# Merging two layer norms, re-cutting weight loads and narrowing a last output tile in a two-layer decode kernel

## The chip, the cores and the metric

The kernel runs on one core of one Trainium2 chip. The metric is the device time of one execution in microseconds (us), as the slowest core shows it; here there is only one. A "profile" is one execution taken by the hardware profiler; "PE" is the matrix engine, "PEld" its weight loads, "DVE" the vector engine, "ACT" the scalar engine, and "SP" the engine that issues the loads.

## The reference, cut to what matters

Two equal layers work on two tokens (`B = 2`) of width `D = 576`. Each layer is attention over a cache of 16384 positions and 32 heads, then a small MLP. Both layers read the same caches and weights.

```python
x = x + attention(LN(x), k_cache, v_cache, wq, wo)   # 2 x 32 heads, 16384 x 128 each
n = LN(x)                                            # input of the MLP block
hs = shift(gelu(LN(n) @ w1)) @ w2                    # of one position only a constant part is left
x1 = n + hs
x  = x + x1 + gelu(LN(x1) @ w3) @ w4                 # w3: 576 x 4608, w4: 4608 x 576
```

With one position per token the shifted term meets only padding, so `hs` doesn't depend on `x`; the kernel computes it once from w2. What matters here: two norms follow each other (`n = LN(x)`, then `LN(n + hs)`), and 1095.6 MB must be read, nearly all of it K and V.

## The kernel before

One SBUF buffer of three "places" takes all that is loaded: K and V of one (batch, head) "unit" fill a place, and between the layers w3, w4 and wq use the same places. An allocator issues a load as soon as the matmuls that read the old content have been queued to signal, in a fixed order. So each load waits for the engines that use what lay there before. Where that wait comes late, the stream of loads runs dry (199 GB/s instead of some 431 in the largest case below); I call this a hole.

```python
W4_PIECES = (1, 4, 4, 2, 1)          # w4 comes in twelfths, in this order, in both layers

def cols(self, ap, t):               # 576 = 4.5 x 128: the last tile takes the LAST 128 columns,
    return ap[:, t*128:(t+1)*128] if t < self.KT - 1 else ap[:, self.D-128:self.D]   # 64 of them twice

def d_matmuls(self, pe, out, w, rhs, first, last):       # one row block of w4, wo or w2
    for t in range(self.KT):                             # KT = 5 output tiles of 128 columns
        ins = pe.matmul(out[:, t*B:(t+1)*B], lhsT=self.cols(w, t), rhs=rhs,
                        start=(first and t == 0), stop=last, skip_group_check=True)

def mlp(self, l):
    self.layernorm(self.xa, "xa", self.xb, "xb")         # n = LN(x): its own sums, Ln/Exp for rstd
    x1 = xb + hs
    self.layernorm(self.x1, "x1", self.xn, "xn")         # LN(x1): sums again
    xsum = xa + x1
    ...                                                  # w3, gelu, then w4: 36 blocks x 5 tiles = 180 matmuls

def ncp(self, l, i): return self.NCH // 2 + 1            # of 16 chunks of K, PE takes 9, DVE 7

rows("wq", 1, self.wq, [third, third + n, third + 2*n, third + unit, third + unit + n])
# attention, layer 2, first units ("early"): exponentials at chunk 3, weighing with V at chunk 5
# ... (cut: loop machinery, softmax, transposes, projection pieces)
```

## Time and profile before

| | before |
|---|---|
| time, median of 4 runs | 2563.47 us (2563.23 to 2563.85) |
| profiled span | 2563.0 us |
| bytes read | 1095.64 MB at 427 GB/s |
| PE, DVE, ACT busy | 64%, 69%, 48% |
| DMA engines busy in the slices | 9 tenths or more, except the last |

The page's slices (40 equal slices of 64 us: busy tenths of the DMA engines, then what they moved) show what bounds the kernel before:

```profile
DMA  9999999999999999999999999999999999999998
GB/s 410 429 431 433 432 430 432 432 431 431 431 431 433 431 432 432 432 430 431 427 378 429 428 433 431 433 431 434 430 431 432 431 433 431 431 433 432 430 431 370
```

No compute engine is near full, but the DMA engines are busy from end to end. The stream moves 429 to 434 GB/s except in the first slice, in slices 20 to 23 (counted from 1) where the layers meet, and in the last. The windows view of before has for each stretch: length, busy us of each engine (number of instructions), granted PE clock (as a share of full speed), DMA share and GB/s.

```profile
core 0: us, PE busy (x) PEld busy (x) DVE busy (x) ACT busy (x) POOL busy (x), PEclk, DMA share, GB/s
1284.00:1290.00 6.00, 4.86 (x163) 4.67 (x163) 0.45 (x4) 0.60 (x3) 0.00 (x0) 0.50 0.63 199
1302.00:1307.00 5.00, 2.95 (x67) 2.66 (x65) 1.09 (x7) 0.50 (x2) 0.00 (x0) 0.50 0.94 357
1308.00:1312.00 4.00, 1.91 (x64) 1.75 (x63) 0.00 (x0) 0.00 (x0) 0.00 (x0) 0.50 1.02 420
1326.00:1330.00 4.00, 2.12 (x25) 1.85 (x25) 3.93 (x7) 2.21 (x3) 0.00 (x0) 0.50 0.89 328
1338.00:1342.00 4.00, 4.00 (x83) 4.00 (x81) 3.93 (x6) 2.15 (x4) 0.00 (x0) 0.50 0.71 233
1500.00:2500.00 1000.00, 635.43 (x14241) 591.50 (x14239) 693.80 (x1005) 484.61 (x765) 0.00 (x0) 0.67 1.00 431
```

Lost stream time is length x (1 - GB/s / 431.8), where 431.8 is the steady rate that I read from the loops. So 199 GB/s over 6 us is a loss of 3.2 us; the stretches at 1302, 1326 and 1338 lose 0.9, 1.0 and 1.8. Between 1500 and 2500 us next to nothing is lost: 0.6 us by the DMA records. The timeline of PE between the layers (start, duration, line, operation, output<-inputs, shapes, count, [idle before <- what ended it]) shows the two norms:

```profile
1278.31 0.29 PE L649 MATMUL misc<-otn,wolast 128*128 128x2 bf16 x5 [0.26 <-DVE otn L843]
1279.06 0.61 PE L579 MATMUL misc<-xa,small 128*128 128x16 f32 x2 [0.46 <-DVE xa L574]
1279.60 0.59 PE L581 MATMUL misc<-xa,small 64*128 64x4 f32 x2
1282.10 0.61 PE L579 MATMUL misc<-x,small 128*128 128x16 f32 x2 [1.91 <-DVE x L574]
1282.64 0.59 PE L581 MATMUL misc<-x,small 64*128 64x4 f32 x2
1284.73 1.12 PE L613 MATMUL sps<-xn,buf 128*128 128x2 bf16 x36 [1.51 <-DVE xn L597]
```

The last projection (1278.31) is followed by a pair of fp32 sums at 1279.06 and another pair at 1282.10; only at 1284.73 can the first w3 matmul start.

```profile
2551.66 1.76 PE L649 MATMUL misc<-prod,buf 128*128 128x2 bf16 x60 [0.45 <-DMA buf<-in_B_w_dram]
2555.82 1.76 PE L649 MATMUL misc<-prod,buf 128*128 128x2 bf16 x60 [2.41 <-DMA buf<-in_B_w_dram]
2557.91 0.96 PE L649 MATMUL misc<-prod,buf 128*128 128x2 bf16 x30 [0.33 <-DMA buf<-in_B_w_dram]
2559.16 0.56 PE L649 MATMUL misc<-prod,buf 128*128 128x2 bf16 x15 [0.29 <-DMA buf<-in_B_w_dram]
```

The last load ends at 2559.11, and only 15 matmuls and some small steps come after it: the output is issued 2.3 us after the last landing. The 60 matmuls of a w4 piece take 1.76 us (29 ns each) and hide between the landings of the pieces. The granted clock in this stretch was 0.50.

### The profile page before, as it was taken

To read this page: it belongs to the slowest core of one execution; us is meant where nothing else is said; L and a number is where in the kernel's file an instruction comes from. 1 tells how busy PE (TensorE), PEld (TensorE's weight loads), DVE (VectorE), ACT (ScalarE), POOL (GpSimd) and SP (SyncE) were. 2 spreads that over 40 slices of the span, in tenths; PEclk is the share of its full clock that TensorE was granted. 3 is DMA by queue.
4 is the path that set the end of the run, shared out by engine and by line. 5 is a ranking of instruction groups with operands and counts; after the bars stand their busy time and mean duration, and the time that the engine had idled before them with its cause. 6 is when DMAs were issued, how large, how long until landed. Compare 5 with 4: busy or idle time off the path is not lost.

```text
span 2563.0 us, 83950 instructions
## 1 busy us (share of the span) xinstructions
PE 1645.9 (64%) x36813; PEld 1532.6 (60%) x36813; DVE 1756.7 (69%) x2592; ACT 1226.3 (48%) x1941; POOL 1.0 (0%) x12
## 2 busy tenths in 40 slices
PE   5666666666566656666668766666666666666666
PEld 5555655566565656655668766556655665565555
DVE  5676767677666766766648867766776767677664
ACT  4544544454445445544436555444544544454442
POOL 0000000000000000000000000000000000000000
PEclk8766666666667666766656667666766666666666
DMA  9999999999999999999999999999999999999998
GB/s 410 429 431 433 432 430 432 432 431 431 431 431 433 431 432 432 432 430 431 427 378 429 428 433 431 433 431 434 430 431 432 431 433 431 431 433 432 430 431 370
DMA packets 46935, 1096.37 MB, mean 428 GB/s; under 512 B 4964, under 2 KB 6056, under 8 KB 11560
## 3 DMA queue, kind: packets, MB, share of 16 engines
q1 hardware_dynamic: 46888, 1095.66, 99.7%
q8 instruction: 39, 0.64, 0.1%
q14 instruction: 8, 0.07, 0.0%
HBM read 1095.64 MB, written 0.00 MB: 427 GB/s over the span
## 4 chain that ended last, share of the span: by engine, by line
DMA 60%; issue 16%; DVE 15%; PE 8%; ACT 0%; SPq 0%; DVEq 0%
DMA buf<-in_A_k_cache_dram 58%; DVE prod L778 12%; PE tps L749 5%; DVE sd L781 3%; PE misc L797 2%; DMA buf<-in_B_w_dram 1%; PE ops L821 1%; DMA buf<-in_A_wq_dram 0%; DVE small L799 0%; PE sps L766 0%; PE sps L613 0%; ACT ktsb L753 0%; SPq L431 0%; PE misc L649 0%; PE misc L579 0%
## 5 line engine op out<-in xcount | busy, mean ns | idle before, releaser
L753 ACT ACTIVATE ktsb<-tps 128x1024 bf16<-128x1024 bf16 x1152 | 1119.4, 1032 | 873.0 <-PE tps L749 868.4
L749 PE MATMUL tps<-ident,buf 128*128 128x128 bf16 x9216 | 903.0, 262 | 623.5 <-DMA buf<-in_A_k_cache_dram 612.3
L749 PEld LDWEIGHTS tps<-ident,buf 128*128 128x128 bf16 x9216 | 727.9, 120 | 651.7 <-DMA buf<-in_A_k_cache_dram 631.7
L781 DVE TENSOR_REDUCE sd<-prod 128x8 f32<-128x1024 bf16 x896 | 1093.2, 1220 | 31.0
L778 DVE TENSOR_TENSOR prod<-buf,qb 128x1024 bf16<-128x1024 bf16 x896 | 610.7, 682 | 11.1 <-DMA buf<-in_A_k_cache_dram 10.2
L821 PE MATMUL ops<-p,buf 128*128 128x1 bf16 x16384 | 463.0, 165 | 69.5 <-DMA buf<-in_A_v_cache_dram 60.8
L821 PEld LDWEIGHTS ops<-p,buf 128*128 128x128 bf16 x16384 | 445.2, 101 | 79.2 <-DMA buf<-in_A_v_cache_dram 69.9
L799 DVE TENSOR_REDUCE small<-misc 128x1 f32<-128x128 f32 x128 | 37.3, 292 | 647.6 <-PE misc L797 647.6
L766 PE MATMUL sps<-qcur,ktsb 128*128 128x1 bf16 x9216 | 395.5, 166 | 112.1 <-ACT ktsb L753 87.7
L766 PEld LDWEIGHTS sps<-qcur,ktsb 128*128 128x128 bf16 x9216 | 345.6, 101 | 176.2 <-ACT ktsb L753 170.8
L733 ACT ACTIVATE qb<-misc 128x128 bf16<-128x128 f32 x130 | 36.0, 277 | 373.6 <-PE misc L730 373.6
L797 PE MATMUL misc<-identS,small 128*128 128x128 f32 x256 | 95.0, 475 | 9.8 <-DVE small L791 9.7
L797 PEld LDWEIGHTS misc<-identS,small 128*128 128x128 f32 x256 | 69.8, 333 | 11.6 <-DVE small L791 11.4
L807 ACT ACTIVATE p<-sps,small 128x72 bf16<-128x72 f32 x128 | 41.6, 325 | 6.7 <-DVE small L799 6.7
L807 ACT ACTIVATE p<-sd,small 128x56 bf16<-128x56 f32 x128 | 44.8, 350 | 0.0
L725 ACT ACTIVATE qcur<-qt 128x1 bf16 (+1 forms) x130 | 29.7, 228 | 20.3 <-DVE qt L659 20.3
L730 PE MATMUL misc<-ident,qcur 128*128 128x128 bf16 x130 | 34.8, 268 | 1.3 <-ACT qcur L725 1.3
L876 PE MATMUL misc<-lpiece,small 128*128 128x16 f32 x28 | 8.5, 385 | 40.9 <-DVE lpiece L874 40.9
L876 PEld LDWEIGHTS misc<-lpiece,small 128*128 128x128 f32 x28 | 7.0, 311 | 43.5 <-DVE lpiece L874 43.5
L787 DVE TENSOR_REDUCE small<-sps 128x1 f32<-128x72 f32 x128 | 28.5, 222 | 0.9 <-PE sps L766 0.9
L807 ACT ACTIVATION_READ_ACCUMULATOR p<-sps,small (+1 forms) x128 | 27.3, 214 | 0.0
L807 ACT ACTIVATION_READ_ACCUMULATOR p<-sd,small (+1 forms) x128 | 26.7, 209 | 0.0
(88 smaller groups left out, 222.2 us busy)
## 6 DMA issues: line engine op xcount, KB each, us to landing
buf<-in_A_k_cache_dram SPq DMA_DIRECT2D x124, 4096.0 KB, 24.3
buf<-in_A_v_cache_dram SPq DMA_DIRECT2D x122, 4096.0 KB, 33.6
buf<-in_A_v_cache_dram SPq DMA_DIRECT2D x5, 2048.0 KB, 22.5
buf<-in_B_w_dram SPq DMA_DIRECT2D x8, 1152.0 KB, 30.8
buf<-in_A_wq_dram SPq DMA_DIRECT2D x8, 1024.0 KB, 8.3
buf<-in_A_wo_dram SPq DMA_DIRECT2D x14, 576.0 KB, 34.6
buf<-in_B_w_dram SPq DMA_DIRECT2D x4, 1728.0 KB, 20.6
buf<-in_A_k_cache_dram SPq DMA_DIRECT2D x3, 2048.0 KB, 10.8
```

The lines of the kernel that those rows point to most:

```text
L725: self.act(lambda a, u: a.activation(out=self.qcur[:, q:q + 1], in_=self.qt[:, bass.ds(u, 1)], func=ACT.Copy), r=["qt"], w=[f"qcur{q}"], u ...
L730: self.pe(lambda pe: pe.matmul(self.misc[:, 0:128], lhsT=bcast(self.qcur[:, q:q + 1], 128), rhs=self.ident[:, :], start=True, stop=True), ...
L733: self.act(lambda a: a.activation(out=self.qb[q][:, :], in_=self.misc[:, 0:128], func=ACT.Copy), r=["P:misc"], w=[f"qb{q}"])
L749: ins = pe.transpose(self.tps[b][:, j * 128:(j + 1) * 128], kt[:, (j0 + j) * 128:(j0 + j + 1) * 128], self.ident[:, :])
L753: self.act(lambda a: a.activation(out=self.ktsb[k][:, :, :].rearrange("p a b -> p (a b)"), in_=self.tps[b][:, :], func=ACT.Copy), r=[f"P:t ...
L766: ins = pe.matmul(self.sps[sp][:, col:col + 1], lhsT=self.ktsb[k][:, j, :], rhs=self.qcur[:, sp:sp + 1], start=True, stop=True)
L778: self.dve(lambda v: v.tensor_tensor(out=self.prod[d][:, :, :], in0=k3, in1=bcast_mid(self.qb[q][:, :], self.CH), op=ALU.mult), r=[*res, f ...
L781: self.dve(lambda v: v.tensor_reduce(out=self.sd[q][:, o:o + self.CH], in_=self.prod[d][:, :, :], axis=AX.X, op=ALU.add), r=[f"prod{d}"], ...
L797: self.pe(lambda pe: pe.matmul(self.misc[:, 128:256], lhsT=bcast(self.m[:, q:q + 1], 128), rhs=self.identS[:, :], start=True, stop=True), ...
L799: self.dve(lambda v: v.tensor_reduce(out=self.bias[:, q:q + 1], in_=self.misc[:, 128:256], axis=AX.X, op=ALU.max, negate=True), r=["P:misc ...
L807: self.act(lambda a, u, c0=c0, c1=c1, src=src: a.activation(out=self.p[q][:, c0:c1], in_=src, func=ACT.Exp, bias=self.bias[:, q:q + 1], sc ...
L821: ins = pe.matmul(self.ops[q][:, 0:1], lhsT=vt[:, j * 128:(j + 1) * 128], rhs=self.p[q][:, h * self.TB + j:h * self.TB + j + 1], start=(h ...
```

## The change

The intent: shorten what lies between the layers, so that the loads that wait for it are issued earlier, and let the stream run through. In the words of the change: both MLP layer norms from one round of sums, w4 and wq in finer pieces at new places, PE takes more chunks of layer 2's first units. (The pieces are finer for layer 1's w4 alone: layer 2's w4 gets a larger first piece, five twelfths, and wq stays in five rows at new places.) The diff, cut to its core:

```diff
-    W4_PIECES = (1, 4, 4, 2, 1)
+    W4_PIECES = ((1, 2, 3, 3, 2, 1), (5, 4, 2, 1))          # by layer
...
-                rows("wq", 1, self.wq, [*(third + k * n for k in range(KT - 2)), third + unit, third + unit + n])
+                free = third + (self.FA - self.W4_PIECES[0][0]) * self.FJ * D
+                rows("wq", 1, self.wq, [free, *(third + k * n for k in range(KT - 1))])
...
+    def layernorms(self):        # sums of xa, xa*hs and xa*xa at once; hs's own sums are made once, with w2
+        ...                      # var(x1) = var(n) + 2 cov(n, hs) + var(hs), from those sums
...
     def d_matmuls(self, pe, out, w, rhs, first, last):
         for t in range(self.KT):
-            ins = pe.matmul(out[:, t * self.B:(t + 1) * self.B], lhsT=self.cols(w, t), rhs=rhs,
+            lo = 0 if t < self.KT - 1 else self.p0                       # p0 = 64
+            ins = pe.matmul(out[lo:128, t * self.B:(t + 1) * self.B], lhsT=w[:, t * 128:(t + 1) * 128 - lo], rhs=rhs,
                             start=(first and t == 0), stop=last, skip_group_check=True)
...
     def ncp(self, l, i):
-        return self.NCH // 2 + 1
+        return self.NCH // 2 + (3, 2)[min(i, 1)] if l == 1 and i < 2 else self.NCH // 2 + 1
...
-                if i >= 1 and c == (3 if early else 4):                  # exponentials
+                if i >= 1 and c == (2 if early else 4):
-                if early and c == 5:                                     # weighing
+                if early and c == 4:
-            if l == 0 and i == 1:
+            if l == 0 and i == 0:
                 self.shift_term()                                        # w2, hs and its sums
...
-        self.dve(lambda v: v.tensor_copy(out=self.xn[:, :, :], in_=self.xa[:, 0, :, :]), r=["xa"], w=["xn"])
+        # (the last cast: layer 2's MLP now writes xn itself)
```

The last output tile of `d_matmuls` is now 64 columns wide, written to partitions 64 to 127. The merged sums need this: the 64 padding rows stay zero, and one fp32 sum over all 128 rows suffices.

## The prediction

> **What bounds it now.** The load stream. The page shows the DMA engines at nine tenths in every slice, 1095.6 MB read at 427 GB/s over 2563.0 us; the inner slices hold 430 to 433. At 431.8 GB/s (my reading of the steady loop) the bytes alone need an estimated 2537 us. The other 26 us are start (4 us), tail, a slow drift, and holes where the two layers meet (slice 20: 378 GB/s). The windows view in small steps puts the holes, as lost stream time, at: 1284 to 1290 us, 3.2 us (w4's second piece waits until two w3 rows have been multiplied, issued 1287.06); 1302 to 1307, 0.8 us (wq waits for w4's buffers, first row issued 1297.26); 1326 to 1330, 1.1 us (K of layer 2's fourth unit waits for VectorE's sixth dot of the first unit, issued 1326.90); 1338 to 1342, 2.1 us (V of that unit waits for the first unit's weighing, issued 1338.92). Sum 7.2 us. Nothing else in the loops is lost: PE, VectorE and ScalarE work there is off the critical path.
>
> **What the change does.**
> 1. One round of sums. The timeline has 5.9 us from the last addition to xa (1278.8) to the first w3 matmul (1284.7), two norms of about 3.0 us each. The merged chain has one fp32 sum (0.6 us instead of two at 1.2, twice), about nine small VectorE steps of 0.2 us and two Ln/Exp pairs of 0.5 us: estimate 3.5 us. Gain 2.3 us, needed only in layer 1; in layer 2's MLP the PE waits for w4's transfers anyway.
> 2. w4's second piece now waits for one w3 row (1.1 us earlier). With 1, issue at about 1283.6 instead of 1287.1; the first hole shrinks to about 0.6 us.
> 3. wq's first row goes to a place free after w4's first piece, the others behind small pieces: issue near 1291, hole gone. In exchange layer 2's K now waits for wq's second and third row; perhaps 0.3 us.
> 4. PE takes 11 and 10 chunks in layer 2's first units; VectorE has 5 and 6 dots of 1.86 us. K's issue comes about 2 us earlier after the unit's start: that hole goes. The weighing comes 2.5 us earlier, but the stream is further ahead too: about 1 us of that hole stays.
> 5. w2 and its statistics at unit 0: some 2 us more of small work in a phase with slack of over 10 us; free. Last cast dropped: 0.2 us at the tail.
>
> **Expected gain.** 7.2 - (0.6 + 0.3 + 1.0) + 0.2 = 5.5 us in mean stream time. [...] the last w4 piece's sixteen signals spread over 5.9 us (2553.2 to 2559.1). [...] I take 0.3 us off.
>
> Predicted 2558.2 us, 8 in 10 between 2556.0 and 2560.8. Faster by over 2%: 0.01; within 2%: 0.985; slower: 0.005.
>
> **Right or wrong in the profile.** Step 1: last xa addition to first w3 matmul about 3.5 us. Step 2: over 350 GB/s in the stretch that held 103 to 174. Step 3: wq's first row issued before w4's last piece has landed. Step 4: VectorE dots of the first unit end about 9.5 us after its first transpose. Steady slices unchanged, PE busy slightly up, VectorE slightly down.
>
> **What would make it wrong.** Engine spread at the tail eating the gain; a new wait at layer 2's K; [...] layer 1's second unit delayed enough to starve the stream.

The sum came to 7.2 - 1.9 + 0.2 = 5.5 us; less the 0.3 us it is 5.2, and 2563.47 - 2558.2 is the 5.3 us that I use below. The reason for the 0.3 us rested on a link between holes and spread that no trace shows. So the 0.3 us are only my guess, beside the 5.9 us of spread that the trace does show.

## More of the kernel before

The weights are the stationary operand (`lhsT`), and the moving operand has two columns (the two tokens). In the trace of before, w4's 128x128 tiles take PE 29 ns each (60 in 1.76 us), so I count PE's time there by weight tiles.

The chain of waits (what ended last, in order of time: start, duration, what) and PE's timeline show the end of the kernel:

```profile
2539.29 19.83 DMA buf<-in_B_w_dram
...
2559.16 0.57 PE misc L649 x15
...
2560.19 0.74 PE misc L561 x5
...
2560.95 0.45 DVE prod L565
```

## The result, and the profile after

The changed kernel is correct and takes 2564.26 us (median of 4 runs, 2563.55 to 2566.16) against 2563.47 us. The ratio is 1.0004, with a 95% interval from 0.9987 to 1.0021: the same. (Ratios here are the mean time of one kernel's fast runs over that of the other's of the same rounds, so not quite the ratio of the medians.) The prediction, 2558.2 us with a range of 2556.0 to 2560.8, missed: none of the 5.3 us came.

Yet the stream did gain. The page's GB/s line and the windows view of after:

```profile
GB/s 409 430 431 433 431 430 433 432 431 432 430 433 432 431 432 431 433 431 431 426 408 431 428 432 430 432 433 431 432 432 430 432 431 431 433 432 431 430 433 341
```
```profile
core 0: us, PE busy (x) PEld busy (x) DVE busy (x) ACT busy (x) POOL busy (x), PEclk, DMA share, GB/s
1284.00:1290.00 6.00, 4.11 (x136) 3.94 (x133) 0.16 (x1) 0.02 (x1) 0.00 (x0) 0.50 0.97 373
1302.00:1307.00 5.00, 3.11 (x45) 2.73 (x42) 1.04 (x7) 0.50 (x2) 0.00 (x0) 0.50 1.01 424
1308.00:1312.00 4.00, 3.02 (x108) 2.88 (x106) 0.10 (x1) 0.00 (x0) 0.00 (x0) 0.50 0.80 275
1326.00:1330.00 4.00, 3.73 (x69) 3.59 (x67) 2.71 (x4) 3.80 (x8) 0.00 (x0) 0.78 1.00 426
1338.00:1342.00 4.00, 3.35 (x71) 3.05 (x69) 2.08 (x6) 3.31 (x5) 0.00 (x0) 1.00 1.07 455
```

Here the hole of 1284 to 1290 went from 199 to 373 GB/s (a loss of 0.8 us instead of 3.2), and those of 1302, 1326 and 1338 are gone. A new one is there, 1308 to 1312, with 275 GB/s instead of 420: 1.5 us. From the trace's DMA records, the loss from 1262 to 1348 us is 4.0 us instead of 8.7. The last landing came at 2554.52 instead of 2559.11, 4.6 us earlier. The merged sums are as fast as predicted:

```profile
1279.09 0.40 PE L693 MATMUL misc<-otn,wolast 128*128 128x2 bf16 x5 [0.26 <-DVE otn L892]
1279.97 0.64 PE L587 MATMUL misc<-xhs,small 128*128 128x30 f32 x2 [0.47 <-DVE xhs L619]
1283.07 1.16 PE L655 MATMUL sps<-xn,buf 128*128 128x2 bf16 x36 [2.47 <-DVE xn L593]
```

From the end of the last addition (1279.70) to the first w3 matmul (1283.07) are 3.4 us, against 5.9 before. So the gain was there until the last load had landed, and was lost after it. The chain of waits and PE's timeline at the end of after:

```profile
2547.21 0.14 issue
2547.34 12.30 PE misc L693 x180
...
2560.65 0.45 DVE prod L573
```
```profile
2542.10 0.64 PE L666 MATMUL sps<-xnh,buf 128*128 128x4 bf16 x18 [0.34 <-DMA buf<-in_B_w_dram]
2547.34 12.29 PE L693 MATMUL misc<-prod,buf 128*128 128x2 bf16 x180 [4.61 <-DMA buf<-in_B_w_dram]
```

PE waits 4.61 us for the first w4 piece, now five twelfths, which lands at 2547.21. Then the 180 matmuls of w4 run in one block of 12.29 us, 68 ns each instead of 29. The last piece landed at 2554.52, in the middle of this block. The granted clock was 0.50 here too, so the clock is not the reason. The end is no longer bound by the load, but by PE: the output is issued 6.6 us after the last landing instead of 2.3.

Why did the same 180 matmuls take so much longer? The tile view of the weight loads lists their shapes, with the least, median and greatest ns of one (it counts every second one of the 360):

```profile
L693 PEld LDWEIGHTS misc<-prod,buf x360: 103/106/126, 1292.0 to 2559.4; 128*128 128x128 bf16 x144, 128*64 128x64 bf16 x36
```

36 of each layer's 180 weight tiles are now 64 columns wide, one in each group of five. The single instructions in the two traces (not a view of the page; start times and gaps, in ns, worked out from the records):

```
before, one group after another:  128 128 128 128 128 | 128 ...    gap to the next start: 26 to 28 each
after, from 2548.005:             128 -49-> 128 -27-> 128 -27-> 128 -95-> 64 -142-> 128   sum 340 per group of five
```

The narrow tile starts 95 ns after the one ahead, and the next wide one 142 ns after it; the one after that takes 49 ns. A group of five takes 340 ns instead of 133. The time is lost at both starts, 95 and 142 ns where 27 are usual; what PE does in it the trace does not show, and whether it is the change of width or the narrow tile itself that costs, a trace of this kernel alone cannot say.

Two theories were to be told apart. Theory A: the narrow tile makes w4 slow, and this eats the stream's gain at the tail. Theory B: the tile is hidden where the stream is the limit, and the gain is lost to the sixteen DMA engines' spread, to new holes, or to the test form.

### The profile page after: what moved, and what is told of

It is laid out like the page before. It is cut to its first block, busy times and chain, and to the rows that moved or that the text cites. A ratio compares the mean times of both kernels' runs of the same rounds, so it can differ in the third digit from the quotient of the medians.

```text
span 2562.7 us, 84020 instructions
## 1 busy us (share of the span) xinstructions
PE 1671.5 (65%) x36847; PEld 1559.0 (61%) x36847; DVE 1751.6 (68%) x2595; ACT 1231.3 (48%) x1944; POOL 1.0 (0%) x12
## 4 chain that ended last, share of the span: by engine, by line
DMA 59%; issue 16%; DVE 13%; PE 10%; ACT 1%; SPq 0%; DVEq 0%
DMA buf<-in_A_k_cache_dram 56%; DVE prod L827 11%; PE tps L798 6%; DMA buf<-in_B_w_dram 1%; DVE sd L830 1%; PE misc L846 1%; DMA buf<-in_A_v_cache_dram 1%; PE ops L870 1%; ACT ktsb L802 1%; PE misc L693 1%; DMA buf<-in_A_wq_dram 0%; PE sps L815 0%; SPq L435 0%; PE sps L655 0%; ACT p L856 0%
## 5 line engine op out<-in xcount | busy, mean ns | idle before, releaser
L693 PE MATMUL misc<-prod,buf 128*128 128x2 bf16 (+1 forms) x360 | 24.6, 179 | 6.6 <-DMA buf<-in_B_w_dram 4.6
L693 PEld LDWEIGHTS misc<-prod,buf 128*128 128x128 bf16 (+1 forms) x360 | 22.4, 111 | 8.8 <-issue 4.7
## 6 DMA issues: line engine op xcount, KB each, us to landing
buf<-in_A_k_cache_dram SPq DMA_DIRECT2D x3, 2048.0 KB, 11.2
```

The costliest lines, as they stand in the source:

```text
L693: ins = pe.matmul(out[lo:128, t * self.B:(t + 1) * self.B], lhsT=w[:, t * 128:(t + 1) * 128 - lo], rhs=rhs, start=(first and t == 0), stop ...
```

## The experiments

The kernels as given wait, inside their loops, for semaphore values held in registers. Such kernels were not admitted to the chip for experiments. So each experiment uses one of three test forms of the same program, and is compared with a before and an after in the same form:

- `_u`: the loops are written out, so that all waits are against constants.
- `_c`: the loops are kept. All engines meet once per turn of two units: SP waits for each engine's count of the turn, takes it back, and gives each a go signal. The semaphores of K, V and wo are taken back to zero before each use.
- `_d`: as `_c`, but the last turn of each loop is written out after it, for a reason that the second job showed.

```diff
 # _u
-        self.s.loops.append((l * U + first, (U - first) // 2, 2, self.WO_PIECE, ...))
 # _c, on SP, once per turn
+            for s, n in subs: eng.wait_ge(sems[s], n)
+            for s, n in subs: eng.sem_inc(sems[s], -n)
+            for e in engines: eng.sem_inc(sems["go_" + e], 1)
 # _d, ahead of all that
+        self.loops = [(first, n - 1, *more) for first, n, *more in self.loops]
```

"Wide" puts the last tile back and zeroes the padding rows ahead of each sum. "Batched" keeps 64 columns, but does all wide tiles of a piece before its narrow ones. "Narrow" is the kernel before with nothing but the narrow tile.

```diff
 # wide: the changed kernel with before's tile
-            lo = 0 if t < self.KT - 1 else self.p0
-            ins = pe.matmul(out[lo:128, ...], lhsT=w[:, t * 128:(t + 1) * 128 - lo], rhs=rhs,
+            ins = pe.matmul(out[:, ...], lhsT=self.cols(w, t), rhs=rhs,
+        # and ahead of each sum over xa or hs:
+        self.dve(lambda v: v.memset(self.xa[0:self.p0, KT - 1, :], 0.0), r=["xa"], w=["xa"])
 # batched: the changed kernel, order of the tiles alone (w4 and the three-head projection)
-                for j in range(n * self.FJ):
+                for ts in (range(KT - 1), (KT - 1,)):
+                  for j in range(n * self.FJ):
 # narrow: the kernel before, with
-            ins = pe.matmul(out[:, ...], lhsT=self.cols(w, t), rhs=rhs,
+            lo = 0 if t < self.KT - 1 else self.p0
+            ins = pe.matmul(out[lo:128, ...], lhsT=w[:, t * 128:(t + 1) * 128 - lo], rhs=rhs,
```

### First job: loops written out

> The kernel before with its loops written out (the looped form waits on registers, which the check refuses). Nothing else differs. All theories: the same computation and the same loads, plus the instruction fetches of some 84,000 instructions: 2590 to 2625 us. The gap from the landing of w4's last piece to the end stays near 3.9 us and w4's last three pieces keep PE waiting on the loads. This run is the baseline of the other written-out kernels.

> The changed kernel with its loops written out. All theories: within about 3 us of before_u (the looped pair differs by 0.8 us). The 180 w4 matmuls of layer 2 take 12.3 us in one run and the end comes 7 to 8 us after w4's last piece has landed, as in the looped one.

> after_u with the last output tile of every down-projection 128 columns wide again (as before), the 64 padded rows zeroed by one memset ahead of the sums. Theory A (the 64-wide matmul between 128-wide ones makes each group of five cost 340 ns instead of 135, and that ate the gain): the 180 w4 matmuls take 5 to 5.6 us, the end comes 4 us after the last landing, the time is 3.5 to 5.5 us below after_u. Theory B (the larger first w4 piece of layer 2, 5 twelfths landing 2.6 us after the gelu is ready, ate it): the time stays within 1.5 us of after_u. Theory C (the loads themselves end late because of the engines' spread): w4's last landing moves and the rest does not follow.

> after_u, still with the 64-wide last tile, but in w4 and in the three-head projection all 128-wide matmuls of a piece come first and its 64-wide ones after them, so that the width changes twice a piece instead of twice a group of five. Theory A1 (the change of width costs): w4 in 5.3 to 6.5 us, time within 1 us of wide_u. Theory A2 (a 64-wide matmul is slow by itself): w4 stays above 9 us, time within 1.5 us of after_u.

| run | median us (range) | ratio to before [95%] | last w4 landing, output issued | after it |
|---|---|---|---|---|
| before_u | 2612.01 (2611.24 to 2612.76) | 1.0189 [1.0172, 1.0206] | 2605.88, 2608.18 | 2.3 us |
| after_u | 2612.25 (2611.27 to 2613.49) | 1.0189 [1.0172, 1.0206] | 2602.79, 2609.36 | 6.6 us |
| wide_u | 2609.24 (2607.16 to 2610.15) | 1.0176 [1.0159, 1.0193] | 2603.67, 2605.77 | 2.1 us |
| batched_u | 2609.39 (2607.63 to 2609.89) | 1.0176 [1.0159, 1.0193] | 2603.78, 2606.14 | 2.4 us |

All are correct, as are all kernels of the later jobs. The kernel before, beside them, took 2563.88 us, so the form itself costs 48 us. Writing the loops out took the instruction fetches from 39 to 288 (before_d, with loops again, has 48). The DMA queue lines of the pages of before and before_u (packets, MB, share of the 16 engines):

```profile
q8 instruction: 39, 0.64, 0.1%
```
```profile
q8 instruction: 288, 4.72, 0.7%
```

An estimate from these lines, 4.08 MB more at the 431.8 GB/s of the steady stream, is 9.4 us. What the rest of the 48 us is was not measured. But the form keeps the picture: after is level with before, its last landing comes 3.1 us earlier, and the tail gives it back. With the tile back to 128 columns, or with the narrow tiles put together, the tail is as short as before's. PE's timeline of batched_u:

```profile
2596.57 2.63 PE L693 MATMUL misc<-prod,buf 128*128 128x2 bf16 x75 [4.59 <-DMA buf<-in_B_w_dram]
2600.66 3.98 PE L693 MATMUL misc<-prod,buf 128*128 128x2 bf16 x105 [1.47 <-DMA buf<-in_B_w_dram]
```

The 75 matmuls of the first piece, 15 narrow ones among them, take 2.63 us instead of the 5.1 that 75 x 68 ns would make. In the records the wide ones start every 27 ns, the first narrow one 95 ns after, and the narrow ones then every 53 ns. So in batched order a group costs 4 x 27 + 53 = 161 ns, and of the 340 ns in the changed order some 179 come with the two changes of width. Narrow tiles are the slower ones even in a row, 53 against 27 ns; whether that is their load is not shown. (A narrow load itself is recorded with a median of 157 ns in batched_u and 125 ns in after, against 104 and 105 for a wide one; but loads overlap, as wide tiles start every 27 ns.) This part, 26 ns a group, is small beside the 179. wide_u and batched_u beat before_u by 2.8 and 2.6 us; since the intervals of the ratios overlap, this job alone does not settle the size. Two expectations missed narrowly: wide_u came 3.0 us below after_u instead of 3.5 to 5.5, and batched_u's w4 took PE 6.6 us instead of at most 6.5.

### Second job: loops kept, one meeting per turn

> The kernel before, with its loops kept but waiting on constants: the engines meet once per two units and the counts are taken back there. The instruction stream is as short as in the kernel before, so the fetches of the written-out kernels are gone. All theories: within 3 us of the kernel before (2561 to 2567 us), because the engines wait for K at each unit's start anyway; w4's last landing about 4 us before the end.

> The changed kernel in the same form. All theories: within 2 us of before_c, w4's 180 matmuls of layer 2 in 12.3 us, w4's last landing about 4 us earlier than in before_c and the end 7.6 us behind it.

> after_c with the 128-wide last tile. Theory A (the changes of width in the down-projections took the gain): w4 in 5 to 5.6 us of PE, the end about 3.3 us behind the last landing, 4 to 6 us below both before_c and after_c, 2557 to 2560 us. Theory C (the spread of the DMA engines took it): 0 to 2 us below after_c.

> before_c with nothing of the change but the 64-wide last tile. Theory A: layer 2's w4 pieces take PE 4.1 us per four twelfths instead of 1.8, so that PE falls behind the landings: w4 ends about 3.3 us later, and between the layers xa comes 3 to 3.5 us later, of which 1 to 2 us reach the load stream: 3 to 6 us above before_c. Theory B (the large first piece is what hurts, the width only in company with it): within 1.5 us of before_c.

| run | median us (range) | ratio to before [95%] |
|---|---|---|
| before_c | 2568.30 (2566.81 to 2568.50) | 1.0017 [1.0003, 1.0030] |
| after_c | 2578.40 (2577.74 to 2580.34) | 1.0056 [1.0043, 1.0070] |
| wide_c | 2570.21 (2570.09 to 2570.81) | 1.0025 [1.0012, 1.0039] |
| before_narrow_c | 2577.78 (2576.96 to 2578.77) | 1.0055 [1.0041, 1.0068] |

The tile alone costs before 9.5 us, and taking it out of after gains 8.2: both more than expected (3 to 6 and 4 to 6), and in both pairs the intervals of the ratios are apart. But before_c came 4.6 us above the kernel before, where under 3 were expected, after_c came 10.1 us above before_c instead of within 2, and wide_c came out 1.9 us *above* before_c, where it should have been 4 to 6 us below. The waits of PE in the last stretch of before_c, and of after_c, show why:

```profile
PE misc L903 <- PEq L248: 8.5, 1, 8.5
```
```profile
PE misc L952 <- PEq L248: 19.3, 1, 19.3
```

PE sat 8.5 us (before_c) or 19.3 us (after_c, and wide_c too) at the gate that ends the loop. SP gives that signal, but SP was held in issuing loads for 25 to 33 us; it got to the signal after three of w4's five last loads in before_c, but only after all four in after_c and wide_c. This is a fault of my test form, not of either kernel. It also laid all 180 w4 matmuls bare behind the gate, so the tile cost its full 7.3 us at the tail (12.32 against 4.97 us in the chains of after_c and wide_c). In before_narrow_c, whose gate wait (8.4 us) is that of before_c, the rest is in the stream: between 1262 and 1348 us it lost 11.2 us instead of 7.9. So with w4 in the pieces of before, the tile costs the stream between the layers too. The form was changed so that nothing waits for SP there.

### Third job: the last turn of each loop written out

> The kernel before with the loops kept and constant waits, like before_c, but with the last turn of each loop written out after the loop. In the earlier form the traces showed that the first small matmul of the last unit's softmax waited 8.5 us (before_c) and 19.3 us (after_c, wide_c) for SP's go signal, while SP was held for 25 to 33 us in issuing DMAs; so its tails say nothing. Here no go signal is needed there. Both theories: 2564.0 to 2566.5 us, output DMA issued 2.0 to 3.0 us after w4's last landing.

> The changed kernel in the same form. Theory A (the 64 columns wide last tile makes w4's 180 matmuls last 12.3 us instead of 5.0, and this eats the stream's gain at the tail): within 1.5 us of before_d, w4's last landing 3.5 to 5 us earlier than in before_d, output DMA issued 6 to 7.5 us after it. Theory B (the tile is hidden where the stream is the limit; the gain is lost to the engines' spread and to new holes): also near before_d, but the last landing is no earlier than before_d's by more than 1.5 us.

> The changed kernel, only the last tile back to 128 columns. Theory A: 3.5 to 5.5 us below before_d and after_d, output DMA issued 2.0 to 2.6 us after w4's last landing, the hole before layer 2's K (wq's second row waits for the MLP's end) under 1 us. Theory B: within 1 us of after_d.

> The changed kernel with the narrow tile kept, only layer 2's w4 pieces back to 1, 4, 4, 2, 1 twelfths (the change has 5, 4, 2, 1). Theory A says that the tail is bound by PE: from the first piece's landing to the end of 180 matmuls. PE idled 4.6 us in the changed kernel until 5 twelfths had landed; with 1 twelfth first it starts after gelu: 2.0 to 2.6 us below after_d, and still 1.5 to 3 us above wide_d. Theory B: within 0.7 us of after_d.

```diff
 # after_w4l2_d, the changed kernel with
-    W4_PIECES = ((1, 2, 3, 3, 2, 1), (5, 4, 2, 1))
+    W4_PIECES = ((1, 2, 3, 3, 2, 1), (1, 4, 4, 2, 1))
```

| run | median us (range) | ratio to before [95%] | stream loss 1262 to 1348 | last w4 landing, output issued | after it |
|---|---|---|---|---|---|
| before_d | 2566.21 (2565.59 to 2566.66) | 1.0009 [0.9996, 1.0023] | 8.6 us | 2559.84, 2562.15 | 2.3 us |
| after_d | 2566.41 (2565.36 to 2567.55) | 1.0009 [0.9995, 1.0022] | 4.7 us | 2556.52, 2563.16 | 6.6 us |
| wide_d | 2561.12 (2560.77 to 2561.76) | 0.9989 [0.9976, 1.0003] | 4.7 us | 2555.93, 2558.03 | 2.1 us |
| after_w4l2_d | 2565.19 (2564.53 to 2566.56) | 1.0006 [0.9992, 1.0020] | 4.1 us | 2555.55, 2561.14 | 5.6 us |

Now before_d and after_d stand to each other as the real kernels do, with the same tails (2.3 and 6.6 us). Theory A's numbers came, but for one: after_d's last landing was 3.3 us earlier than before_d's, where 3.5 to 5 were expected. With the tile alone put back, wide_d is 5.3 us faster than after_d and 5.1 us faster than before_d, with ranges that lie 3.6 us or more apart. (The intervals of the ratios still touch, at 0.9995 to 1.0003; that the tail is what differs is read from the traces.) Stream loss and landing of wide_d are those of after_d within what single traces scatter (see the fourth job); what differs clearly is the tail. Theory B wanted wide_d within 1 us of after_d, and it falls. wide_d's chain of waits and PE timeline end like before's:

```profile
2536.66 19.27 DMA buf<-in_B_w_dram
...
2555.98 0.57 PE misc L801 x15
```
```profile
2548.78 2.14 PE L801 MATMUL misc<-prod,buf 128*128 128x2 bf16 x75 [4.63 <-DMA buf<-in_B_w_dram]
2552.82 1.55 PE L801 MATMUL misc<-prod,buf 128*128 128x2 bf16 x52 [1.91 <-DMA buf<-in_B_w_dram]
2554.67 1.86 PE L801 MATMUL misc<-prod,buf 128*128 128x2 bf16 x53 [0.30 <-issue]
```

The load is the last wait again, and PE idles between pieces. One expectation missed: the hole before layer 2's K should have been under 1 us in wide_d; it was 1.1 us by the DMA records. In after_d it was 1.3 us, so the tile has little to do with this hole.

after_w4l2_d gained 1.2 us in the median (2.0 in the profiled runs; the ranges overlap), less than the 2.0 to 2.6 expected, and stayed 4.1 us above wide_d, where 1.5 to 3 were expected. PE's timeline says why:

```profile
2545.76 1.09 PE L800 MATMUL misc<-prod,buf 128*128 128x2 bf16 x15 [2.01 <-DVE prod L830]
2548.29 11.36 PE L800 MATMUL misc<-prod,buf 128*128 128x2 bf16 x165 [1.44 <-DMA buf<-in_B_w_dram]
```

The small first piece lets only 15 matmuls run early (1.09 us). The other 165 wait for the second piece (landed 2548.24), which is hardly earlier than the large first one. So the larger first piece cost about the time of those 15 matmuls. That the tail is bound by PE is confirmed; the waiting time of 4.6 us was not all to be had.

### Fourth job: the single steps, and one improvement

The cause was found, but not whether each term of the predicted sum was right. Each of these kernels is wide_d with one step undone, or with one more.

> wide_d (the changed kernel with the last tile back to 128 columns) with one more edit: layer 2's first loaded K comes in four quarters instead of a half and two quarters, so its first piece waits for one row of wq to have been multiplied, not for two. In wide_d the stream lost 1.1 us between 1310 and 1314 us, and K's first piece was issued at 1310.71, 2.5 us after the matmuls of the row before had ended (1308.2). Theory C (the row of wq that K's place waits for is what empties the stream there): K's first issue near 1308.3, loss in the stretch 1308 to 1316 under 0.4 us, time 0.6 to 1.3 us below wide_d, so 2559.8 to 2560.5. Theory D (that stretch is lost to the end of the MLP, the sums before wq, whatever K waits for): same loss, time within 0.4 us of wide_d.

> wide_d with two norms, each with its own sums, one after the other, in the MLP; all else as in wide_d. Last addition to xa until first w3 matmul: near 6 us instead of 3.5. If the prediction's first step is right, layer 1's hole near 1285 grows by 2.0 to 2.6 us and the time by as much (2563.1 to 2563.8); in layer 2 nothing is lost, as PE waited 4.6 us for w4 there. If other holes take it up: less than 1.2 us.

> wide_d with layer 1's w4 in the pieces of the kernel before (1, 4, 4, 2, 1 twelfths) and wq's rows for layer 2 in the places of before (steps 2 and 3 of the prediction undone; layer 2's w4 stays). The prediction's terms: hole after the first w4 piece +2.6 us, wq's hole +0.8, K's new hole -0.3 (measured in wide_d: 1.1). Sum with the measured hole: 2.0 to 2.6 us slower than wide_d (2563.1 to 2563.7). If less than 1 us: the places bought little, and the merged sums did most.

> wide_d with PE's share of layer 2's first two units back to 9 of 16 chunks and the exponentials and weighing at their old places (step 4 undone). The prediction's terms: hole of K +1.1 us, of V +1.1 us (one of its 2.1 us was to remain). In wide_d neither hole is left (losses of 1326 to 1330 and 1336 to 1342 together under 0.3 us), so the undone step should cost up to 3.2 us, and more than before's, as the stream is further ahead: 2.2 to 4 us slower than wide_d (2563.3 to 2565.1). If under 1.5 us, those holes had come from the stream's place in time, not from the share of chunks.

```diff
 # wide_k2_d: layer 2's first loaded K in quarters
-                kv("K", l, i, {(1, 2): (2, 1, 1), (1, 3): (2, 2)}.get((l, i)))
+                kv("K", l, i, {(1, 2): (1, 1, 1, 1), (1, 3): (2, 2)}.get((l, i)))
 # wide_ln2_d: layernorms() as two norms, each with its own sums (one fp32 sum each, not before's two)
 # wide_places_d
-    W4_PIECES = ((1, 2, 3, 3, 2, 1), (5, 4, 2, 1))
+    W4_PIECES = ((1, 4, 4, 2, 1), (5, 4, 2, 1))
-                rows("wq", 1, self.wq, [free, *(third + k * n for k in range(KT - 1))])
+                rows("wq", 1, self.wq, [*(third + k * n for k in range(KT - 2)), third + unit, third + unit + n])
 # wide_chunks_d: ncp() is NCH // 2 + 1 everywhere; exponentials at chunk 3, weighing at chunk 5
```

| run | median us (range) | ratio to before [95%] | stream loss 1262 to 1348 | against wide_d: stream, time |
|---|---|---|---|---|
| wide_k2_d | 2561.19 (2560.60 to 2563.16) | 0.9990 [0.9976, 1.0004] | 4.3 us | -0.4, +0.1 us |
| wide_ln2_d | 2563.14 (2561.59 to 2563.47) | 0.9996 [0.9982, 1.0009] | 6.5 us | +1.8, +2.0 us |
| wide_places_d | 2562.35 (2561.37 to 2562.91) | 0.9994 [0.9980, 1.0008] | 5.4 us | +0.7, +1.2 us |
| wide_chunks_d | 2563.54 (2563.01 to 2565.61) | 1.0000 [0.9986, 1.0014] | 6.2 us | +1.5, +2.4 us |

These ran in another job than wide_d, on another chip, where the kernel before took 2563.46 instead of 2563.87 us, and the 95% intervals overlap. So the times are good to about half a microsecond. The stream losses are from one trace each, and they scatter too: up to 1308 us wide_d, wide_k2_d and wide_chunks_d are the same program, yet from 1262 to 1308 us they lost 3.2, 2.2 and 2.4 us. So a difference under about 1 us shows nothing, and wide_d's trace, which lost most there, makes the others look better than they are. What the steps are worth has to be read where the kernels differ:

- The two norms in a row lost 4.5 us up to 1308, that is 1.3 to 2.3 us more than those three, and 2.0 us in time: the first step was right, near the lower end of what was expected. From the last addition to the first w3 matmul took 5.0 us, not near 6 as expected (wide_d 3.5, before 5.9), so this edit undoes some three fifths of the step.
- The chunks lost 3.8 us from 1308 to 1348, 2.3 us more than wide_d, in holes at 1326 and 1336 to 1342 that came back, and 2.4 us in time. That is the 2.2 us of the prediction's terms; the whole window shows only 1.5 because of the scatter before 1308.
- The places fell short: 2.0 to 2.6 us were expected, and 1.2 us came in time. In wide_places_d wq's hole came back (0.9 us at 1302 to 1306), but K's hole of 1.1 us went away in exchange. From 1284 to 1294 us it lost 2.5 us, against 2.2 in wide_d, and 1.4 and 1.6 in wide_k2_d and wide_chunks_d, so what the small pieces saved is not clear of the scatter.

The windows view of wide_d, and then of wide_k2_d, tells what K's hole was made of, and where its end led:

```profile
1310.00:1312.00 2.00, 0.69 (x26) 0.60 (x23) 0.00 (x0) 0.00 (x0) 0.00 (x0) 0.50 0.98 338
1312.00:1314.00 2.00, 1.55 (x48) 1.44 (x48) 0.00 (x0) 0.00 (x0) 0.00 (x0) 0.50 0.84 326
1336.00:1338.00 2.00, 1.11 (x17) 1.11 (x17) 1.97 (x3) 0.19 (x2) 0.00 (x0) 0.50 1.17 492
```
```profile
1310.00:1312.00 2.00, 0.55 (x20) 0.46 (x18) 0.00 (x0) 0.00 (x0) 0.00 (x0) 0.50 1.01 391
...
1336.00:1338.00 2.00, 0.59 (x7) 0.59 (x6) 1.97 (x4) 0.55 (x1) 0.00 (x0) 0.50 0.74 295
```

With K in quarters its first piece was issued at 1307.64 instead of 1310.71, and the hole from 1308 to 1316 shrank from 1.2 to 0.6 us (under 0.4 was expected): that fits theory C, that K waited for wq's rows. But the time did not move, where 0.6 to 1.3 us were expected. The stream met a new hole at V (1336 to 1338, 295 GB/s); from 1308 to 1348 us, where alone the two kernels differ, it lost 2.1 us against 1.5, so in all nothing was gained. That it met V's wait because it was further ahead is likely, not shown. In its profiled run, the slowest of its five, the last load's sixteen signals also spread over 8.5 us instead of 6.7. Whether the spread grows when holes go stays open: it was 5.9 us before, 6.1 after, 6.6, 7.4 and 6.7 us in before_d, after_d and wide_d, and 10.1 us in wide_u.

No kernel in the four jobs beats wide_d. It is 5.1 us faster than before_d in the same form, and 2.8 us faster than the kernel before itself (2563.87 us in the same job; the ratio's interval, 0.9976 to 1.0003, just includes 1), although its form costs about 2.3 us (before_d against before). Worked out from these, an estimate for the changed kernel in its own form with only the tile put back is 2563.5 - 5.1 = 2558.4 us.

## Why the prediction was wrong

In the prediction's own terms, what failed is the path at the tail. Its sum counts stream time alone and lets the end follow the last landing, since "in layer 2's MLP the PE waits for w4's transfers anyway". After the change PE waited for the first of these transfers only, until 2547.21, and then was itself the limit for 12.29 us. The cause is a line of the diff that the prediction didn't have. Its list of what the change does has five steps and no word on `d_matmuls`, whose last tile went from 128 to 64 columns. The diff shows it in two lines and it looks like less work: half the columns in every fifth tile. In the trace it is 2.5 times the time per group (340 against 133 ns), 7.3 us per 180 matmuls. Put back alone, it gives 5.3 us in after_d against wide_d, as much as the whole predicted gain.

Point by point:

- **What bounds the kernel: right up to the tail.** The stream sets the time in both layers (DMA share 1.00 and 431 GB/s between 1500 and 2500 us), and 4.6 us of the predicted 5.3 net stream gain arrived (last landing 2554.52 instead of 2559.11). The prediction then took the tail as fixed, 2.3 us behind the last landing. In after it was 6.6 us, since PE's 12.29 us from the first piece became longer than what was left to load.
- **Step 1, the merged sums: right.** 3.4 us were measured, 3.5 predicted; undone for three fifths, the step costs 2.0 us of time (2.3 predicted for the whole).
- **Step 2, w4's second piece: right in the profile, its worth not shown.** 373 GB/s were reached where over 350 were predicted. But with wide_places_d undoing it, the stretch from 1284 to 1294 us lost 2.5 us, against 1.4 to 2.2 in three kernels with the small pieces: 0.2 to 1.1 us, about as much as these three differ. What the pieces bought in the real kernel's own form, apart from the merged sums, stays open.
- **Step 3, wq's place: right for its own hole, wrong for K's.** wq's first row was issued at 1293.07, before w4's last landing (1300.30), and the hole went. K's new hole was 1.5 us in after (windows view) and 1.1 us in wide_d (DMA records), against 0.3 predicted. This term was mis-sized, and the new hole outweighs the 0.8 us that wq's hole had cost. In after, w4's slow matmuls also delayed the norm ahead of wq (w4's last piece landed at 1300.30, its last matmul ended at 1304.26); in wide_d the landing of wq's rows was enough to make the hole.
- **Step 4, the chunks: right.** The first unit's dots ended 9.9 us after its first transpose (9.5 predicted). Layer 2's K was issued at 1321.75 instead of 1326.90, V at 1333.21 instead of 1338.92. Both holes went, although 1.0 us of V's was to remain. Undone, it costs 2.3 us of stream after 1308 us and 2.4 us of time, where 2.2 were predicted.
- **Step 5: free, as predicted**, in so far as the losses before 1262 us are equal (4.9 and 5.0 us). The larger first piece of w4 in layer 2, which the prediction did not mention either, cost about 1.2 us as long as the tile was narrow. In wide_d PE waits for the later pieces anyway, so it should cost nothing there; that was not run.
- **"PE busy slightly up": a warning not followed.** PE's busy time rose by 25.6 us. The narrow tile explains about all of it: 13.4 us in the two layers' w4 (24.6 us against 11.2), 10.3 in the pieces of the attention's output projection (19.9 against 9.7), which the stream does not show (next to nothing is lost between 1500 and 2500 us in either kernel), and 2 in its smaller uses; the merged sums took some 4 us off. With the tile put back, PE's busy time fell from 1674.4 us (after_d) to 1648.7 (wide_d). (The transposes took 8.7 us more in after, but their busy time scatters between 898 and 915 us in kernels that do equally many, before_d and before_c.) Costing this line of the diff from the page would have shown that a busy time of PE was still to be placed.
- **The engines' spread eating the gain**, named as what could make it wrong, was not the cause: 5.9 us before, 6.1 after.

## What to carry to other kernels

Cost every line of a diff, also those that seem to remove work: a matmul tile of half the width, put as every fifth among full ones, made the group take 2.5 times as long here (340 against 133 ns), and the same narrow tiles put together cost a fifth more (161 ns). Look again at slack behind a stream after each change: here w4's matmuls hid between the landings at 29 ns each, and became the bound at 68 ns each with a last landing 4.6 us earlier. A single trace is a thin measure of a small term: three runs of the same code lost 2.2 to 3.2 us in one stretch. A gain on the stream should be checked at two points, at the last landing and at the end, for the two parted here: 4.6 us earlier at the landing, 0.8 us later in the median time.
